# Attention and spectral layers on one core: the second addition behind the last low part, the norms' squares on ScalarE, wo's staging a step earlier

## The chip, the cores and the metric

The kernel runs on one core of a Trainium2 chip. A core has five engines that matter here: TensorE (PE in the profile; PEld is its weight load, which overlaps the products), VectorE (DVE), ScalarE (ACT), GpSimd (POOL) and SyncE (SP), which here issues nearly all DMA transfers. Each engine works its own instructions off in order and waits on semaphores for the others. The metric is the time of one execution on the device, in microseconds (us).

## The reference

The input x is 2048 x 1024 (one batch), and four blocks are applied to it, each with a residual: attention, spectral, attention, spectral.

```python
def _A_ref(x, wqkv, wo):                       # 32 heads of 32
    qkv = (x @ wqkv).reshape(B, S, 3, H, Dh)   # then q, k, v
    scores = einsum("bhqd,bhkd->bhqk", q, k) * Dh ** -0.5
    p = softmax(scores)
    return einsum("bhqk,bhkd->bhqd", p, v).reshape(B, S, D) @ wo
def _B_ref(x, w_r, w_i):
    return irfft2(rfft2(x) * (w_r + 1j * w_i), s=(S, D))
x = x + _A_ref(_layernorm(x), wqkv, wo)
x = x + _B_ref(_layernorm(x), w_r, w_i)
x = x + _A_ref(_layernorm(x), wqkv, wo)
x = x + _B_ref(_layernorm(x), w_r, w_i)
```

## The kernel before

The change touches the attention block, which is run twice (layer 0 and layer 1). Values that need more than 16 bits are kept as two halves of type f16: the high part, a rounded copy (ScalarE, line 167), and the low part, the rest (VectorE, line 168). The function `split` makes both. A product of two such values takes three products on TensorE.

The 32 heads are taken in 8 groups g of 4 heads. For a group, the queries stand in 4 chunks c of 512 and the keys in 16 tiles kt of 128, so that the loop over u = (c, kt) has 64 steps a group. A step does this:

- `S`: 12 score products (line 552) into two score tiles named s. The pool of score tiles has three buffers, which are taken in turn; besides S, the sum z at a chunk's end (line 581) and the norms' product (line 354) take one.
- two exponentials on ScalarE (line 556) of 128x1024 each, from s into p; p has eight buffers.
- on even steps `PV` (line 562) for the last two steps' p.
- `add` for one step: two additions on VectorE (line 575; at kt = 1 the form of line 573), which add p into two accumulators. They are late by a pair of steps.
- at a chunk's end `fin`: z from the accumulators on TensorE (line 581), then a transpose, a reciprocal and a scaling on VectorE (582 to 588); some steps later `out`: a cast on ScalarE (594), a subtraction on POOL (595) and a store to od on SP (597).
- on odd steps a piece of the filler: the projections for the next groups. `qk_chunk` makes a chunk of queries or keys: 24 products (line 337) into the projection buffer named x, of which there is one, then `split` into Q, or into K, which lies in the tile that the profile names R. `v_tiles` (line 381) makes v in the same buffer. So the next chunk's first product waits for both halves of the last one's split.

The exponentials' bias comes from a bound on the scores: each q or k chunk is squared (line 341, on POOL, into sq), and when four chunks are done `norms` sums the squares over a head's rows on TensorE (line 354, into a score buffer), VectorE takes the maximum (line 356, into mqk), and POOL works the bias out from it.

The weights of the next projection are loaded beside (line 248, into wst, three buffers) and split (into wqk or wv); in layer 0 alone VectorE also takes their largest value (lines 257 and 258). In group 6 wo is loaded and split in 16 pieces through the same three buffers (`load_wo`, line 417).

The order on TensorE and ScalarE in the loop is the order in which the code is written (`manual_schedule`). On VectorE, POOL and SP a scheduler sets the order. The name R stands for one large region that holds keys, values and the accumulators, and big for another one with the normalised input and wo.

## Time and profile before

| | |
|---|---|
| median of 3 runs | 3925.26 us (3918.09 to 3928.21) |
| profiled execution | 3923.33 us, span 3921.4 us |
| mean clock of TensorE | 0.984 |
| attention loop of layer 0, without its end | about 135 to 1300 us |
| attention loop of layer 1, without its end | about 2100 to 3240 us |

The page's first part gives each engine's busy time and its share of the span. A view of windows gives the same for a stretch of time, with the clock that TensorE was granted in it (PEclk, 1 is full speed). A view of waits names, for an engine, the line that waited, the engine and line it waited for, the sum, the number and the longest. In a timeline a row has the start, the duration, the engine, the line and operation with tile names (out<-in) and the number of instructions; in brackets the engine's idle time before it and what ended it. SPq is SP's queue, on which a row is the issue of a transfer.

### The profile page before, as it was taken

The page shows a single profiled execution, that of the slowest core. Times are in us where ns is not written, and L with a number is a line of the kernel's source. Part 1 is how long each engine was busy: PE and PEld are TensorE (multiplying, and loading weights), DVE is VectorE, ACT ScalarE, POOL GpSimd, SP SyncE. Part 2 cuts the span into 40 slices and gives each one's busy share as a digit, 9 for nine tenths or more (in the row PEclk, how much of TensorE's full clock was granted, in tenths as well). Part 3 has the DMA queues.
Part 4 walks back from the last instruction along what each step waited for, and adds up shares of the span by engine and source line. Part 5 has one row for each costly group of instructions (what it writes and reads, how often), then busy time and mean ns, then how long its engine had stood idle before and what let it go on. Part 6 is the DMA issues. An engine that isn't in the chain of part 4 may idle for free.

```text
span 3921.4 us, 79594 instructions
## 1 busy us (share of the span) xinstructions
PE 3742.8 (95%) x32948; PEld 1641.1 (42%) x32948; DVE 3183.4 (81%) x3781; ACT 2894.6 (74%) x3561; POOL 639.2 (16%) x575
## 2 busy tenths in 40 slices
PE   6999999999999999989989999999999999999798
PEld 4322432342234233368853334233422432333698
DVE  6689898989898887866666998899898888788455
ACT  4677887888788765557756888888888787665486
POOL 1111011101110200014321220122021102000143
PEclk9999999999999999999999999999999999999899
DMA  8000000000000211144170000000000002111333
GB/s 202 15 17 18 12 12 17 17 12 20 12 23 7 75 67 68 60 145 137 61 172 15 17 17 12 12 17 25 7 18 17 17 12 90 57 68 55 131 113 107
DMA packets 165142, 194.08 MB, mean 49 GB/s; under 512 B 74784, under 2 KB 120480, under 8 KB 163744
## 3 DMA queue, kind: packets, MB, share of 16 engines
q1 hardware_dynamic: 164624, 188.82, 15.4%
q8 instruction: 260, 4.26, 0.4%
q14 instruction: 114, 0.93, 0.1%
q10 hardware_dynamic: 144, 0.07, 0.0%
HBM read 123.83 MB, written 48.23 MB: 44 GB/s over the span
## 4 chain that ended last, share of the span: by engine, by line


## 5 line engine op out<-in xcount | busy, mean ns | idle before, releaser
L556 ACT ACTIVATE p<-s,bias 128x1024 f32<-128x1024 f32 x2048 | 2168.3, 1111 | 593.1 <-PE s L552 581.6
L575 DVE TENSOR_TENSOR R<-R,p 128x1024 f32<-128x1024 f32 x1792 | 2145.9, 1250 | 150.8 <-ACT p L556 146.7
L562 PE MATMUL o<-p,R 128*32 128x512 f32 x8192 | 985.1, 598 | 0.0
L337 PE MATMUL x<-big,wqk 128*128 128x512 f16 x2880 | 693.1, 387 | 28.0 <-DVE R L168 13.9
L552 PEld LDWEIGHTS <-R 32*128 32x128 f16 x12288 | 231.3, 92 | 782.1 <-issue 666.0
L337 PEld LDWEIGHTS <-wqk 128*128 128x128 f16 x3072 | 279.4, 99 | 472.0 <-issue 183.4
L552 PE MATMUL s<-R 32*128 32x512 f16 x6144 | 432.4, 379 | 19.3 <-ACT p L556 15.8
L552 PE MATMUL s<-Q,R 32*128 32x512 f16 x6144 | 432.9, 378 | 11.3 <-ACT p L556 10.6
L562 PEld LDWEIGHTS o<-p,R 128*32 128x32 f32 x8192 | 213.7, 109 | 524.5 <-issue 523.9
L595 POOL TENSOR_TENSOR ohl<-zt,ohl 128x512 f16<-128x512 f32 x62 | 180.0, 2903 | 1472.3 <-ACT ohl L594 1472.3
L381 PE MATMUL x<-wv,big 128*128 128x256 f16 x2688 | 325.7, 278 | 45.8 <-DMA big<-hl 33.2
L381 PEld LDWEIGHTS <-big 128*128 128x128 f16 x3072 | 294.4, 99 | 150.5 <-issue 77.7
L573 DVE SCALAR_TENSOR_TENSOR R<-p 128x1024 f32<-128x1024 f32 x128 | 153.9, 1203 | 198.8 <-ACT p L556 198.5
L341 POOL TENSOR_TENSOR sq<-R 128x512 bf16<-128x512 f16 x96 | 144.8, 1508 | 694.5 <-ACT R L167 691.3
L440 PE MATMUL x<-big 128*128 128x512 f16 x1008 | 228.0, 380 | 0.0
L440 PEld LDWEIGHTS <-big 128*128 128x128 f16 x1344 | 126.7, 98 | 177.6 <-issue 35.4
L885 DVE TENSOR_TENSOR H<-G,H 128x512 f16<-128x512 f32 (+1 forms) x68 | 47.4, 697 | 103.3 <-ACT H L884 103.2
L837 PE MATMUL ps<-cbi,H 128*128 128x256 f16 (+1 forms) x792 | 100.4, 275 | 6.1 <-ACT H L884 3.8
L830 ACT COPY U<-ps 64x256 f32<-64x256 f32 (+1 forms) x272 | 97.0, 357 | 8.5 <-PE ps L837 3.4
L830 ACT COPY B<-ps 64x256 f32<-64x256 f32 (+1 forms) x272 | 97.0, 356 | 6.7 <-PE ps L837 2.4
L341 POOL TENSOR_TENSOR sq<-Q 128x512 bf16<-128x512 f16 x32 | 44.9, 1403 | 323.8 <-ACT Q L167 323.8
L837 PE MATMUL ps<-cb,big 128*128 128x256 f16 x780 | 96.3, 273 | 0.0
(417 smaller groups left out, 3017.2 us busy)
## 6 DMA issues: line engine op xcount, KB each, us to landing
wst<-in_wp SPq DMA_DIRECT2D x96, 256.0 KB, 3.1
R<-y SPq DMA_DIRECT2D x32, 512.0 KB, 5.3
w<-in_w SPq DMA_DIRECT2D x60, 256.0 KB, 2.6
od<-ohl SPq DMA_DIRECT2D x56, 256.0 KB, 2.4
big<-od SPq DMA_DIRECT2D x16, 896.0 KB, 7.0
y<-R SPq DMA_DIRECT2D x20, 512.0 KB, 2.6
R<-in_x SPq DMA_DIRECT2D x16, 512.0 KB, 5.3
wst<-in_wo SPq DMA_DIRECT2D x32, 256.0 KB, 3.0
```

Source lines behind the costliest of these rows:

```text
L337: nc.tensor.matmul(ps, a, b, start=d == 0 and i == 0, stop=d == 7 and i == 2)
L341: nc.gpsimd.tensor_tensor(nrm[ph][:, c], t[:, 0], t[:, 0], op=ALU.mult)
L381: nc.tensor.matmul(ps[:, j], l, r, start=d == 0 and i == 0, stop=d == 7 and i == 2)
L440: nc.tensor.matmul(p, a, b, start=start and d == ds[0] and i == 0, stop=stop and d == ds[-1] and i == 2)
L552: nc.tensor.matmul(s[h // 2][:, h % 2], K[g][r, a, kt * 128:kt * 128 + 128], Q[g][r, b, c * 512:c * 512 + 512], start=i == 0, stop=i == 2)
L556: nc.scalar.activation(p, s[hf], AF.Exp, bias=bias[g], scale=SCALE / (SQ * SQ))
L562: nc.tensor.matmul(O[g, c][32 * h:32 * h + 32], V[g][:, kt, 32 * h:32 * h + 32], P[g, c, kt, h // 2][:, h % 2], start=kt == 0, stop=kt == ...
L573: nc.vector.scalar_tensor_tensor(acc[hf], P[g, c, 0, hf], 1e-34, p, op0=ALU.add, op1=ALU.add)
L575: nc.vector.tensor_add(acc[hf], acc[hf], p)
L595: eng.tensor_tensor(t[:, 1], r, t[:, 0], op=ALU.subtract)
L830: nc.scalar.copy(ov[64 * r:64 * r + 64, a0:a0 + m, x], tl[64 * x:64 * x + 64, :m, r])
L837: nc.tensor.matmul(out, l, r, start=k == 0, stop=k == len(mm_) - 1)
```

## The change

Three things are done in the attention loop.

1. `split` returns its VectorE instruction, and `qk_chunk` keeps it in the list lows. On odd steps, `add` is recorded under `issue_after` with the last of them: the two additions of that step stand behind the last low part in VectorE's order. No semaphore is added by that, since both are on VectorE.
2. The squares of line 341 are made on ScalarE with the activation Square, directly behind the chunk's high part. 56 of them stand in each layer's loop and 8 in each layer's prologue, 128 in all.
3. `load_wo` loads three pieces before its first yield, and one call of it is made when four chunks of filler are left, ahead of the calls that split.

```diff
 def split(nc, hi, lo, src, scale):
     nc.scalar.activation(hi, src, AF.Copy, scale=scale)
-    nc.vector.scalar_tensor_tensor(lo, src, scale, hi, op0=ALU.mult, op1=ALU.subtract)
+    return nc.vector.scalar_tensor_tensor(lo, src, scale, hi, op0=ALU.mult, op1=ALU.subtract)
...
-        split(nc, t[:, 0], t[:, 1], ps, SQ / (SX * SW))
-        nc.gpsimd.tensor_tensor(nrm[ph][:, c], t[:, 0], t[:, 0], op=ALU.mult)
+        lows.append(split(nc, t[:, 0], t[:, 1], ps, SQ / (SX * SW)))
+        nc.scalar.activation(nrm[ph][:, c], t[:, 0], AF.Square)
...
         load(0)
         load(1)
+        load(2)
+        yield
         for i in range(16):
-            load(i + 2)
+            if i:
+                load(i + 2)
...
-    left, parts, rests = 16, 20, list(range(12))
+    left, parts, rests = 17, 20, list(range(12))
...
                 for w in late[:1]:
-                    add(*w)
+                    with tc.issue_after(lows[-1].ins) if kt % 2 else ExitStack():
+                        add(*w)
...
+                if g == NG - 2 and todo == 4 and left == 17:
+                    next(lwo)
+                    left -= 1
```

What this makes of the order is seen at three places. The line numbers of the changed kernel are up to 8 higher: 573, 575 and 594 become 576, 578 and 597, and 556 and 566 become 559 and 569.

VectorE in layer 0, where the loop goes over from keys to v (386 us in the trace of before). wv is the weights' low part, wm and fw the largest value of the weights, R<-x the low part of the last key chunk, mqk the maximum of the norms. Before:

```order
L575 TENSOR_TENSOR R<-R,p 128x1024 x4
L168 SCALAR_TENSOR_TENSOR wv<-wst,wv 128x4x128 x2
L575 TENSOR_TENSOR R<-R,p 128x1024 x2
L257 TENSOR_REDUCE wm<-wst 128x1 x2
L258 TENSOR_TENSOR fw<-fw,wm 128x1 x2
L575 TENSOR_TENSOR R<-R,p 128x1024 x6
L168 SCALAR_TENSOR_TENSOR R<-x,R 128x512
L575 TENSOR_TENSOR R<-R,p 128x1024 x2
L356 TENSOR_REDUCE mqk<-s 128x1
L575 TENSOR_TENSOR R<-R,p 128x1024 x14
```

and after the change:

```order
L578 TENSOR_TENSOR R<-R,p 128x1024 x4
L168 SCALAR_TENSOR_TENSOR wv<-wst,wv 128x4x128 x2
L578 TENSOR_TENSOR R<-R,p 128x1024 x2
L257 TENSOR_REDUCE wm<-wst 128x1 x2
L258 TENSOR_TENSOR fw<-fw,wm 128x1 x2
L578 TENSOR_TENSOR R<-R,p 128x1024 x4
L168 SCALAR_TENSOR_TENSOR R<-x,R 128x512
L578 TENSOR_TENSOR R<-R,p 128x1024 x4
L356 TENSOR_REDUCE mqk<-s 128x1
L578 TENSOR_TENSOR R<-R,p 128x1024 x14
```

The low part has moved ahead of two additions; mqk has as many additions ahead of it as before.

VectorE in layer 0, in a group's query chunks (243 us in the trace of before). Before:

```order
L168 SCALAR_TENSOR_TENSOR wqk<-wst,wqk 128x512 x2
L575 TENSOR_TENSOR R<-R,p 128x1024 x2
L257 TENSOR_REDUCE wm<-wst 128x1 x2
L258 TENSOR_TENSOR fw<-fw,wm 128x1 x2
L575 TENSOR_TENSOR R<-R,p 128x1024 x6
L168 SCALAR_TENSOR_TENSOR Q<-x,Q 128x512
L575 TENSOR_TENSOR R<-R,p 128x1024 x8
L168 SCALAR_TENSOR_TENSOR Q<-x,Q 128x512
L575 TENSOR_TENSOR R<-R,p 128x1024 x2
L356 TENSOR_REDUCE mqk<-s 128x1
```

and after the change:

```order
L168 SCALAR_TENSOR_TENSOR wqk<-wst,wqk 128x512 x2
L578 TENSOR_TENSOR R<-R,p 128x1024 x2
L257 TENSOR_REDUCE wm<-wst 128x1 x2
L258 TENSOR_TENSOR fw<-fw,wm 128x1 x2
L578 TENSOR_TENSOR R<-R,p 128x1024 x4
L168 SCALAR_TENSOR_TENSOR Q<-x,Q 128x512
L578 TENSOR_TENSOR R<-R,p 128x1024 x8
L168 SCALAR_TENSOR_TENSOR Q<-x,Q 128x512
L578 TENSOR_TENSOR R<-R,p 128x1024 x4
L356 TENSOR_REDUCE mqk<-s 128x1
```

Again each low part stands two additions earlier, and mqk where it stood.

ScalarE in layer 0 around a chunk's end (oc and ohl belong to the output of a chunk of queries; 332 us in the trace of before is the place of the cast and the high part behind it). Before:

```order
L566 COPY oc<-o 128x512
L556 ACTIVATE p<-s,bias 128x1024 x2
L167 ACTIVATE R<-x 128x512
L556 ACTIVATE p<-s,bias 128x1024 x8
L594 CAST ohl<-zt 128x512
L167 ACTIVATE R<-x 128x512
L556 ACTIVATE p<-s,bias 128x1024 x4
```

and after the change:

```order
L569 COPY oc<-o 128x512
L559 ACTIVATE p<-s,bias 128x1024 x2
L167 ACTIVATE R<-x 128x512
L341 ACTIVATE sq<-R 128x512
L559 ACTIVATE p<-s,bias 128x1024 x8
L597 CAST ohl<-zt 128x512
L167 ACTIVATE R<-x 128x512
L341 ACTIVATE sq<-R 128x512
L559 ACTIVATE p<-s,bias 128x1024 x4
```

Each high part has a square directly behind it and ahead of the exponentials. On SP the loop's rows, the loads of wo among them, stand in the same order before and after; in layer 0's prologue one load of weights has moved ahead of two transposing transfers.

## The prediction

> **What bounds the kernel now.** I read the page's busy times first, then TensorE's busy time and clock over the attention loops of the two layers, then what TensorE waited for there, then the timeline at the longest waits.

> ```profile
> PE 3742.8 (95%) x32948; PEld 1641.1 (42%) x32948; DVE 3183.4 (81%) x3781; ACT 2894.6 (74%) x3561; POOL 639.2 (16%) x575
> core 0: us, PE busy (x) PEld busy (x) DVE busy (x) ACT busy (x) POOL busy (x), PEclk, DMA share, GB/s
> 28.00:135.00 107.00, 94.18 (x623) 58.29 (x624) 49.15 (x103) 42.97 (x59) 12.79 (x16) 0.95 0.55 116
> 135.00:1300.00 1165.00, 1144.01 (x10732) 400.17 (x10728) 1045.96 (x1055) 938.86 (x997) 140.37 (x100) 0.99 0.05 15
> 2100.00:3240.00 1140.00, 1129.79 (x10738) 397.05 (x10740) 1021.64 (x987) 939.95 (x999) 197.01 (x101) 1.00 0.05 16
> ```

> TensorE sets the time: in layer 0's loop it stands still 21 of 1165 us, in layer 1's 10 of 1140. VectorE is 90% and ScalarE 81% busy there, so both have room on average, and little of it locally. What can be won is TensorE's idle time and its clock. Layer 0's idle time, in the loop's window, and layer 1's, from 2080 to 3640 us:

> ```profile
> PE x L337 <- DVE R L168: 6.6, 3, 2.5
> PE x L337 <- DVE Q L168: 6.4, 3, 2.2
> PE x L381 <- DVE R L168: 6.0, 3, 2.0
> PE s L552 <- DVE mqk L356: 0.6, 1, 0.6
> PE s L354 <- ACT p L556: 0.6, 3, 0.2
> ...
> PE s L552 <- ACT p L556: 13.1, 13, 6.7
> PE s L354 <- POOL sq L341: 6.5, 3, 2.2
> PE s L552 <- DVE mqk L356: 2.6, 4, 0.7
> ```

> Layer 0 waits nine times, 19.0 us in all, for a low part (L168) of the single projection buffer x: three times each for a key part (R), a query part (Q), and a key part ahead of v's projection (L381). Layer 1 hardly has that wait, since its weights aren't measured by L257; it waits three times for POOL's squares. One low-part place, around 243 us:

> ```profile
> 234.75 7.74 DVE L575 TENSOR_TENSOR R<-R,p 128x1024 f32<-128x1024 f32 x6
> 237.80 0.60 ACT L167 ACTIVATE Q<-x 128x512 f16<-128x512 f32 x1
> 242.41 0.68 DVE L168 SCALAR_TENSOR_TENSOR Q<-x,Q 128x512 f16<-128x512 f32 x1
> 243.14 4.39 PE L337 MATMUL x<-big,wqk 128*128 128x512 f16 x12 [2.19 <-DVE Q L168]
> ...
> 243.10:246.50 3.40, 3.36 (x8) 1.13 (x8) 3.40 (x4) 0.01 (x1) 0.00 (x0) 0.50 0.02 5
> 1127.20:1130.60 3.40, 3.40 (x22) 1.08 (x24) 3.40 (x4) 0.73 (x1) 1.07 (x1) 0.51 0.00 0
> ```

> The high part is there at 238.40, the low part stands behind six additions of 1.29 us and ends at 243.09. TensorE loses 2.19 us and then runs a stretch of 3.40 us at half clock, which costs another 1.7. Seven of the nine places have such a stretch (the first and the last are shown): 11.9 us, which is the 0.01 that the window's mean clock of 0.99 lacks on 1165 us.

> **Part 1, the low part ahead of two additions.** By the order, the low part moves ahead of one step, two additions of about 1.25 us, so 2.5 us: as much as the longest of the nine waits. All nine go as waits for L168. What is late next is the maximum of the norms, L356, which keeps its place among the additions; it frees a score buffer that the next S wants. Its price is seen at such waits above: 0.6 and 2.6 us in 1 and 4 times, at most 0.7 each.

> Key and query chunks of layer 0 (six places): 6.6 + 6.4 idle and five half-clock stretches of 1.7 come back, 21.5 in all; three of them then run into L356 at 0.7, so 19.4 us. Bounds: 21.5 if L356 is never late, 10 if it takes the whole of the three query places (6.4 and three stretches).

> The three places ahead of v's projection come out otherwise:

> ```profile
> 381.49 2.12 ACT L556 ACTIVATE p<-s,bias 128x1024 f32<-128x1024 f32 x2
> 383.99 0.40 PE L354 MATMUL s<-sq,bones 128*32 128x512 bf16 x4
> 385.69 0.68 DVE L168 SCALAR_TENSOR_TENSOR R<-x,R 128x512 f16<-128x512 f32 x1
> 386.29 2.34 DVE L575 TENSOR_TENSOR R<-R,p 128x1024 f32<-128x1024 f32 x2
> 386.42 3.57 PE L381 MATMUL x<-wv,big 128*128 128x256 f16 x16 [2.03 <-DVE R L168]
> 388.56 0.68 DVE L356 TENSOR_REDUCE mqk<-s 128x1 f32<-128x512 f32 x1
> 389.92 0.83 PE L552 MATMUL s<-Q,R 32*128 32x512 f16 x12
> ```

> With the low part early L381 begins at 384.4, but the S behind it needs the buffer of L356, which ends at 389.24 whether the low part stands before or behind the two additions. S began at 389.92, so about 0.6 us is won at each place, 1.8 in all, of 6.0 and two stretches (9.4). Bounds 0 and 9.4; I take the low value, because both rows are on VectorE and their sum stays.

> Each addition moved is later by 0.68 us. The additions' readers are the exponentials that take their buffer (eight of them, four pairs' halves deep) and the sum z of a chunk; no row above shows an exponential waiting for an addition, so I cost that at nothing. If the cover went, it would be 0.68 at a chunk's end.

> **Part 2, squares on ScalarE.** 128 operations leave POOL. Three waits of layer 1 go:

> ```profile
> 2338.13 2.02 POOL L341 TENSOR_TENSOR sq<-R 128x512 bf16<-128x512 f16 x1
> 2340.20 0.38 PE L354 MATMUL s<-sq,bones 128*32 128x512 bf16 x1 [2.16 <-POOL sq L341]
> 2341.15 0.68 DVE L356 TENSOR_REDUCE mqk<-s 128x1 f32<-128x512 f32 x1
> ```

> That is 6.5 us and one half-clock stretch, 8.2. Behind it S meets L356 again, at 0.7 three times; and at three places of layer 1 the low part, by the order, now waits for its high part with the additions behind it, and they push L356 by about as much: 8.2 - 2.1 - 2.1 = 4.0. Bounds: 8.2, and -2 if L356 takes it all.

> The price is on ScalarE. A square is not in the trace there; the nearest row is a cast of the same tile, 0.62 us, and I take 0.6. It stands behind the high part and ahead of the exponentials, so those end 0.6 us later until ScalarE has made it up. Who waits for them: S and the norms' product, which take the score buffers (three).

> ```profile
> L594 ACT CAST ohl<-zt 128x512 f16<-128x512 f32 x64 | 39.5, 617 | 0.0
> ...
> 333.18 3.25 ACT L556 ACTIVATE p<-s,bias 128x1024 f32<-128x1024 f32 x3
> 334.46 0.82 PE L552 MATMUL s<-Q,R 32*128 32x512 f16 x12
> ```

> Where a high part stands alone, TensorE has 0.38 us before L354: the exponentials end at 383.61, L354 starts at 383.99. With 0.6 it loses 0.22. Twelve norms in each loop, some with less room: I take 0.24 each, 24 of them, 5.8 us. Where the cast of the output stands beside the high part, the first exponential ends at 334.27 (a third of 3.25 after 333.18) and the S begins at 334.46, with 0.16 left for its second buffer: it loses 0.44, six times a layer, 5.4 us. For the remaining 76 I cost them at nothing: ScalarE is idle 226 of the loop's 1165 us, six times the 34 us of a loop's 56 squares, and makes a square up before it is missed; if that cover goes, it is rival 2. Near wo's splits ScalarE has no room: 1.3 for two more. So 12.5 us is lost. Bounds: 0, and 0.6 for each of the 112 of the loops, 67 us, if ScalarE's 0.6 us always come through; I stay near the low end, since the rows above leave 0.16 us or more at each kind of place.

> **Part 3, wo's staging.** One load is issued a step earlier. At the place that hurts:

> ```profile
> 1277.81 0.95 SPq L417 DMA_DIRECT2D wst<-in_wo  x2
> 1322.89 6.67 SPq L417 DMA_DIRECT2D wst<-in_wo  x4
> ...
> 1344.74 9.31 POOL L595 TENSOR_TENSOR ohl<-zt,ohl 128x512 f16<-128x512 f32 x1 [9.80 <-ACT ohl L594]
> 1352.96 0.68 DVE L168 SCALAR_TENSOR_TENSOR Q<-x,Q 128x512 f16<-128x512 f32 x1
> 1354.08 0.38 SPq L597 DMA_DIRECT2D od<-ohl  x1
> 1354.55 0.91 SPq L417 DMA_DIRECT2D wst<-in_wo  x2
> 1357.62 0.63 ACT L167 ACTIVATE big<-wst 128x512 f16<-128x512 f32 x1 [6.88 <-DMA wst<-in_wo]
> 1359.30 1.46 PE L552 MATMUL s<-R 32*128 32x512 f16 x10 [6.95 <-ACT p L556]
> ```

> The first three loads were issued 40 us before the fourth anyway; by the order, SP's rows and the splits of wo stay what they were. The wait of 6.95 us (6.7 in layer 1) comes otherwise: POOL's subtraction takes 9.31 us beside the additions and ends at 1354.05, just behind a low part; the store of od waits for it on SP's queue, the later load of wo waits behind that store, ScalarE's split for the load, and the exponentials stand behind the split. The load itself is worth 0 here (at most 0.9, its issue time). But part 1 moves the low part at 1352.96 ahead of two additions, and I let the subtraction end 2.2 us earlier with it: twice 2.2, 4.4 us. Bounds: 0, and 13.7 and two half-clock stretches (17) if the wait goes.

> **Prologue.** Sixteen squares beside 43 us of ScalarE in 107: bounds -2 and 9.6 (all on the path); I take 1 us lost.

> **The sum.** 19.4 + 1.8 + 4.0 + 4.4 - 12.5 - 1 = 16.1 us. The profiled execution took 3923.33 us (span 3921.4), 1.9 under the median of 3925.26. 3923.3 - 16.1 = 3907 us.

> **A rule on the clock.** The rows show a half-clock stretch of 3.4 us behind waits of only 2 us. [...] As a rival: stretches stay, six of them for 10.2 us, time 3917. Chance 0.05.

> **The rivals.**
> 1. L356 takes over the query places and layer 1's whole: the gain falls by 9 and 6, to about 3921. For it: 90% of VectorE, and L356 keeps its place. Against: at most 0.7 us was ever waited for it. Chance 0.18.
> 2. Slower: the square delays exponentials by its length at every chunk, and S waits each time. 112 x 0.6 = 67 lost against 28.6 won otherwise (19.4 + 1.8 + 4.0 + 4.4 - 1): 3923 + 38 = 3962; at half of that price, 3928. It decides from 0.26 us a square on (28.6 / 112), or 0.36 for slower by over 0.3%. For it: high part and square come in a row, 1.2 us ahead of two exponentials of 2.12. Against: the three score buffers. Chance 0.15.
> 3. All waits go: no L356 behind the low part, wo's wait gone with its stretches, squares hidden: 19.0 + 11.9 + 8.2 + 17 = 56 off, 3867; with half the squares' price 3873. Against: L356 did not move. Chance 0.13.
> 4. The change does not do what it says (the low part still waits for its high part): 3923. Against: high parts end 4 us before low parts begin at 243 us. Chance 0.04.

> **How the numbers follow.** My forecast, some 3893 to 3915, has 0.45. 0.3% is 12 us, about what a measurement of this kernel can tell from no change, so faster means under 3913.5. Faster: nearly all of the forecast (0.43) and rival 3 (0.13), 0.56. Same: the rest of it, rivals 1 and 4 and the clock rule, 0.29. Slower: rival 2, 0.15. The range takes rival 3 in nearly to its end and rival 2 up to the half price and a little: 3876 to 3934.

> **What would show it.** Right: no wait of x for L168 above 0.5 us in layer 0, PEclk there 1.00, waits of S for mqk at some nine to twelve places of 0.7, L354's wait for POOL gone and replaced by 0.2 to 0.4 for exponentials, the load of wo landing 2 us earlier and the wait behind it 4.7 instead of 6.95. Wrong: waits of S for p at each chunk (rival 2), mqk waits of 2 us (rival 1), additions that exponentials wait for.

## The result and the profile after

The changed kernel takes 3925.12 us (median of 12 runs, 3921.78 to 3928.68); the kernel before, run beside it, 3925.32 (12 runs). The ratio is 1.0007, with a 95% interval of 1.0000 to 1.0015: no change that can be measured. The forecast was 3907. The profiled execution has a span of 3925.2 us.

The page and the two windows of the loops, after:

```profile
PE 3750.5 (96%) x32948; PEld 1644.3 (42%) x32948; DVE 3128.1 (80%) x3781; ACT 2964.6 (76%) x3689; POOL 448.9 (11%) x447
...
135.00:1300.00 1165.00, 1145.23 (x10760) 400.86 (x10756) 1022.67 (x1056) 967.18 (x1050) 74.76 (x49) 1.00 0.05 15
2100.00:3240.00 1140.00, 1131.62 (x10696) 398.46 (x10696) 992.42 (x982) 962.25 (x1046) 101.02 (x49) 1.00 0.05 16
```

POOL has lost 190 us of work and ScalarE has gained 70; layer 0's clock has gone from 0.99 to 1.00. TensorE stands still nearly as long as before (20 and 8 us in the two windows, against 21 and 10). What it waits for is another thing (first layer 0's loop, then layer 1 from 2080 to 3640 us):

```profile
PE s L555 <- DVE mqk L356: 10.2, 9, 2.3
PE s L584 <- DVE R L578: 4.5, 4, 1.6
PE s L584 <- ACT p L559: 2.4, 2, 1.2
PE s L555 <- ACT p L559: 1.3, 6, 0.4
PE s L354 <- ACT p L559: 1.0, 6, 0.2
...
PE s L555 <- ACT p L559: 14.6, 23, 4.6
PE s L555 <- DVE mqk L356: 7.7, 11, 1.0
...
PE s L354 <- ACT p L559: 1.3, 8, 0.2
```

All nine waits for L168 in layer 0 are gone, 19.0 us, and POOL's three in layer 1, 6.5 us. In their place stand waits of S for the norms' maximum mqk (0.6 before, now 10.2, in layer 0), and waits of the sum z (L584) for the additions and for the exponentials from which it takes its score buffer, 6.9 us. VectorE's own waits, which a reader would not look at while VectorE is not the bound, show what changed; the first row is of before, then layer 0 and layer 1 after:

```profile
DVE R L168 <- ACT R L167: 0.8, 3, 0.3
```

```profile
DVE R L168 <- ACT R L167: 36.2, 23, 2.3
...
DVE zt L585 <- PE s L584: 22.7, 13, 2.7
DVE Q L168 <- ACT Q L167: 8.9, 9, 1.7
...
DVE R L168 <- ACT R L167: 42.0, 29, 2.3
...
DVE zt L585 <- PE s L584: 22.7, 13, 2.7
DVE Q L168 <- ACT Q L167: 14.6, 12, 2.2
```

A low part that is placed ahead of two additions stands at the head of VectorE's queue before ScalarE has made its high part, and VectorE idles: 45 us at 32 places in layer 0 and 57 us at 41 in layer 1, where it had idled under 1. The order has a second effect of this kind. At 13 chunk ends in each of the two windows the first additions of the next chunk, which stood ahead of z's transposition, stand behind a low part now; the transposition is at the head of the queue instead, and VectorE idles 22.7 us for z. VectorE's idle time as a whole rose less, from 119 to 142 us in layer 0's window and from 118 to 148 in layer 1's, since it waits less for exponentials (108 us before and 65 after in layer 0); what has changed is where it stands idle. One such place in a group's second chunk, and the z behind it, after:

```profile
160.27 0.69 DVE L168 SCALAR_TENSOR_TENSOR R<-x,R 128x512 f16<-128x512 f32 x1 [1.28 <-ACT R L167]
...
174.14 2.10 PE L584 MATMUL s<-R,ones 128*32 128x512 f32 x8 [0.94 <-DVE R L578]
```

VectorE loses 1.28 us at 160; the chunk's last additions, which VectorE meets 12 us later behind the splitting and measuring of the weights, are late, and z waits 0.94 us where it had started without idle time. Some of z's waiting is hidden in its own row: its eight products take 1.06 us where nothing holds them and 2.10 here. In layer 1, where no wait of z is listed, its products took 34.1 us in all before and take 38.0 now.

### The profile page after: what moved, and what is told of

The parts are those of the page before. It is cut to its first block, busy times and chain, and to the rows that moved or that the text cites. A ratio compares the mean times of both kernels' runs of the same rounds, so it can differ in the third digit from the quotient of the medians.

```text
span 3925.2 us, 79400 instructions
## 1 busy us (share of the span) xinstructions
PE 3750.5 (96%) x32948; PEld 1644.3 (42%) x32948; DVE 3128.1 (80%) x3781; ACT 2964.6 (76%) x3689; POOL 448.9 (11%) x447
## 4 chain that ended last, share of the span: by engine, by line
## 5 line engine op out<-in xcount | busy, mean ns | idle before, releaser
L578 DVE TENSOR_TENSOR R<-R,p 128x1024 f32<-128x1024 f32 x1792 | 2090.6, 1225 | 121.6 <-ACT p L559 117.9
L337 PE MATMUL x<-big,wqk 128*128 128x512 f16 x2880 | 682.4, 382 | 7.6 <-ACT wqk L167 5.4
L337 PEld LDWEIGHTS <-wqk 128*128 128x128 f16 x3072 | 276.0, 98 | 445.4 <-issue 150.9
L598 POOL TENSOR_TENSOR ohl<-zt,ohl 128x512 f16<-128x512 f32 x62 | 165.5, 2669 | 2456.4 <-ACT ohl L597 2456.4
L381 PE MATMUL x<-wv,big 128*128 128x256 f16 x2688 | 322.3, 276 | 39.6 <-DMA big<-hl 33.2
L381 PEld LDWEIGHTS <-big 128*128 128x128 f16 x3072 | 293.4, 99 | 139.6 <-issue 67.9
L168 DVE SCALAR_TENSOR_TENSOR R<-x,R 128x512 f16<-128x512 f32 x88 | 60.6, 689 | 99.2 <-ACT R L167 99.2
L167 ACT ACTIVATE R<-x 128x512 f16<-128x512 f32 x88 | 52.7, 599 | 56.1 <-PE x L337 55.7
```

The lines of the kernel that those rows point to most:

```text
L168: return nc.vector.scalar_tensor_tensor(lo, src, scale, hi, op0=ALU.mult, op1=ALU.subtract)
L337: nc.tensor.matmul(ps, a, b, start=d == 0 and i == 0, stop=d == 7 and i == 2)
L381: nc.tensor.matmul(ps[:, j], l, r, start=d == 0 and i == 0, stop=d == 7 and i == 2)
L578: nc.vector.tensor_add(acc[hf], acc[hf], p)
L598: eng.tensor_tensor(t[:, 1], r, t[:, 0], op=ALU.subtract)
```

## The experiments

My theory after this comparison, called A (C in the later runs, with what the first ones had added): part 1 costs by VectorE's idle time at the head of its queue. Its rival B: the squares on ScalarE eat what part 1 wins. Each run is compared with runs of the kernel before on the same chip. Differences in us are between the two medians; the ratio is worked out from all runs of both kernels, and the two can differ by some 5 us (for part 1 alone the medians are 22 us apart, and 0.0068 is 27).

**Each part alone.** Part 1 alone is the change without the edits of line 341 and of `load_wo`:

```diff
-                    add(*w)
+                    with tc.issue_after(lows[-1].ins) if kt % 2 else ExitStack():
+                        add(*w)
```

> Part 1 alone (squares stay on POOL, wo's loads as before). Theory A (head of the queue): the low part now stands at the head of VectorE's queue and VectorE idles there for the high part, 45 us in layer 0's loop and 57 in layer 1's of the changed kernel; the additions behind it come late and with them the maximum mqk and the sum z. Then these waits stand here too, with the squares on POOL: layer 0 wins 19.0 of waits and 11.9 of clock and loses about 9.6 (mqk), 6.9 (z) and 5 (clock), layer 1 loses about 5 and keeps POOL's 6.5, the wait at wo shrinks by 2.4 in each layer: net about -9, 3916. Theory B (the squares on ScalarE eat the gain): no z wait, few mqk waits, 19.4 + 1.8 + 4.4 - 2 = 24 won: 3902.

Measured: 3948.56 us, ratio 1.0068 (1.0055 to 1.0081), 22 us slower. Its waits of TensorE in layer 0's loop, and two of VectorE's:

```profile
PE s L552 <- DVE mqk L356: 13.9, 9, 2.9
PE s L581 <- DVE R L575: 5.0, 4, 1.4
PE x L337 <- DVE R L168: 4.1, 3, 1.4
PE x L381 <- DVE R L168: 3.1, 3, 2.2
PE x L337 <- DVE Q L168: 3.1, 3, 1.0
PE s L581 <- ACT p L556: 2.6, 2, 1.3
...
DVE R L168 <- ACT R L167: 26.4, 17, 2.3
...
DVE Q L168 <- ACT Q L167: 8.7, 9, 1.8
```

B falls: the z and mqk waits stand here with the squares on POOL. A's waits are there, but its 3916 is missed by 32 us: half of the waits for the low part stay as well (10.3 of 19.0), and layer 1 waits 14.2 us for mqk.

Part 2 alone:

```diff
-        nc.gpsimd.tensor_tensor(nrm[ph][:, c], t[:, 0], t[:, 0], op=ALU.mult)
+        nc.scalar.activation(nrm[ph][:, c], t[:, 0], AF.Square)
```

> Part 2 alone. Theory A: POOL's waits of layer 1 go (6.5 and a half-clock stretch, less 2 for mqk), the additions beside POOL's squares get shorter by 0.3 and the low parts of layer 0 come some 0.4 earlier at nine places, and ScalarE's price is about 10 to 12: net between 0 and +4, 3925 to 3929; nine waits for L168 of 1.6 to 2.1 stay in layer 0. Theory B: the whole gain of part 1 (24) is eaten here, 3940 or more, with waits of S for exponentials at many chunks.

Measured: 3903.98 us, ratio 0.9950 (0.9938 to 0.9962), 22 us faster. Both theories missed it.

```profile
PE x L337 <- DVE Q L168: 3.6, 3, 1.3
PE x L337 <- DVE R L168: 3.4, 3, 1.9
PE s L354 <- ACT p L556: 2.4, 10, 0.4
PE x L381 <- DVE R L168: 2.1, 3, 0.7
PE s L552 <- DVE mqk L356: 1.9, 3, 0.6
```

With VectorE's order untouched, the nine waits for the low part fall from 19.0 to 9.1 us, and not one half-clock stretch is left in the loop, where seven were (the loop's clock is 1.00 instead of 0.99). So the squares on POOL were a cause of the low parts' lateness. POOL's three waits of layer 1 are gone as well. In the profiled executions layer 0, from its first exponential to its last, is 14.9 us shorter than before, and layer 1 is 3.8 shorter. The price on ScalarE is there too (2.4 us for L354 instead of 0.6), and smaller than what is won. Parts 1 and 2 alone, +22 and -22, add up to the change's zero; that this is no rule, the pairs below show.

Part 3 alone (the call of `load_wo` at four chunks, not printed here, is in it):

```diff
+        load(2)
+        yield
         for i in range(16):
-            load(i + 2)
+            if i:
+                load(i + 2)
```

> Part 3 alone. Both theories: the loads were issued 40 us ahead of the first split anyway and SP's order is the same, so 0: within 1 us of before, and the wait of 6.95 at the wo place unchanged.

Measured: 3926.17 us, ratio 0.9999 (0.9990 to 1.0008). The wait of S at the wo place, in a window from 1320 to 1400 us, of this kernel:

```profile
PE s L555 <- ACT p L559: 6.7, 1, 6.7
```

It stays, and part 3 is worth nothing.

**Half the dose of part 1.** Only the second addition of the odd step, and the next step's two, stand behind the low part, so that it moves ahead of one addition; squares on POOL.

```diff
-    def add(g, c, kt):
+    def add(g, c, kt, low=None, first=0):
         for hf in range(2):
+            with tc.issue_after(low.ins) if low is not None and hf >= first else ExitStack():
...
-                    add(*w)
+                    low = lows[-1] if kt % 2 else low
+                    add(*w, low, kt % 2)
```

> Part 1 at half its dose: only the second half of the odd step's addition and the next step's stand behind the low part, so it moves ahead of one addition, not two (squares on POOL, wo as before). Theory A: VectorE's idle time for high parts falls to a third or less, the z wait goes and mqk waits shrink to 1 at v and 0 to 0.3 elsewhere; the waits for L168 in layer 0 fall from 2.1 to about 0.9 each and most half-clock stretches go with them: 8 + 3 + 3 left of 30.9, about 3908, faster than the full dose. Theory B: between before and part 1 alone, about 3913.

Measured: 3916.66 us, ratio 0.9983 (0.9975 to 0.9992). The sign of the dose turns: one addition wins 10 us (7 by the ratio), two lose 22. VectorE idles 15 us for high parts in layer 0 instead of 35. The size is A's missed by 9 us, since 12.9 us of waits for L168 stayed and mqk and z took 9.8.

**The price of a square on either engine.** The squares of the first three of four chunks are made twice, once on ScalarE (on top of part 2) and once on POOL (on top of the kernel before). The second writes the same values, and nobody waits for it alone.

```diff
+        for _ in range(2 if c < 3 else 1):
+            nc.scalar.activation(nrm[ph][:, c], t[:, 0], AF.Square)
```

> Part 2 alone, with every square of the first three of four chunks made twice on ScalarE (42 more of 0.6 us in each loop; the second writes the same values). If the price of a square is its delay of the exponentials less the 0.15 to 0.4 us of room at the score buffers, a second one finds no room: 84 times some 0.4, 3904 + 35 = 3939. If ScalarE's idle time takes squares up however they fall: 3904 + 3.

Measured: 3941.71 us, ratio 1.0042 (1.0028 to 1.0055): 38 us above part 2 alone, 0.45 for each of the 84 squares more in the loops (12 more stand in the prologues), as expected. S waits for exponentials much more often (layer 0, then layer 1 with the wo place):

```profile
PE s L553 <- ACT p L557: 9.4, 23, 0.8
...
PE s L553 <- ACT p L557: 25.0, 39, 6.4
```

That is 17 us more than in part 2 alone (1.3 and 15.7 us there); the rest of the 38 isn't listed as a wait for exponentials.

> The kernel before, with every square of the first three of four chunks made twice on POOL (no consumer waits for the second). Theory C, that POOL's squares cost by slowing VectorE's additions beside them: each second square costs VectorE 0.3 to 0.6 us, 84 of them, the low parts of layer 0 are later by 0.5 to 1 us at nine places and the wait at wo gets longer: +8 to +15, 3934 to 3941. If only the latency of the last square mattered (POOL's waits of layer 1): 0, 3926.

Measured: 3960.14 us, ratio 1.0095 (1.0081 to 1.0110), 36 us slower, more than twice the expected size. The waits in layer 0 and the page's row of the additions:

```profile
PE x L337 <- DVE R L168: 12.5, 6, 4.2
PE x L337 <- DVE Q L168: 11.5, 3, 4.0
PE x L382 <- DVE R L168: 6.7, 3, 2.4
...
L576 DVE TENSOR_TENSOR R<-R,p 128x1024 f32<-128x1024 f32 x1792 | 2189.2, 1274 | 147.4 <-ACT p L557 143.2
```

The same row of before, and of part 2 alone:

```profile
L575 DVE TENSOR_TENSOR R<-R,p 128x1024 f32<-128x1024 f32 x1792 | 2145.9, 1250 | 150.8 <-ACT p L556 146.7
```

```profile
L575 DVE TENSOR_TENSOR R<-R,p 128x1024 f32<-128x1024 f32 x1792 | 2107.6, 1227 | 170.5 <-ACT p L556 167.1
```

So a square on POOL costs VectorE's additions: 38 us less of them without the squares, 43 us more with 96 of the 128 squares doubled, while VectorE's order in the two loops is the same in all three kernels. That a mean moves by 23 ns says little; what decides is that a square follows a high part, and so its delay falls on the additions just ahead of that chunk's low part, which TensorE waits for. At the place of 243 us the six additions ahead of the low part took 7.74 us in the kernel before, where one square ran on POOL beside them. The same six in part 2 alone, with no square on POOL, and in this kernel, with two:

```profile
233.68 6.90 DVE L575 TENSOR_TENSOR R<-R,p 128x1024 f32<-128x1024 f32 x6
...
237.51 8.58 DVE L576 TENSOR_TENSOR R<-R,p 128x1024 f32<-128x1024 f32 x6
```

Each square costs VectorE 0.84 us there. The six take 6.90 us with no square on POOL, 7.74 with one and 8.58 with two; by what the square makes them longer is not shown.

**Only the last square.**

```diff
+        if c == 3:
+            nc.scalar.activation(nrm[ph][:, c], t[:, 0], AF.Square)
+        else:
+            nc.gpsimd.tensor_tensor(nrm[ph][:, c], t[:, 0], t[:, 0], op=ALU.mult)
```

> Only the last of four chunks' squares on ScalarE, the others stay on POOL. By latency alone (POOL's waits of layer 1, 6.5 and a half-clock stretch) 8 won less some 3 for the squares at the norms: 3921. If most of part 2's gain of 22 is the additions' freedom from POOL, a quarter of that (4) comes on top at most: 3917 to 3921, and the nine low-part waits of layer 0 stay near 2 us. If the last square carries everything: 3904.

Measured: 3912.86 us, ratio 0.9969 (0.9958 to 0.9981), 11 us faster, half of part 2 with a quarter of its squares. The wait of v's product (L384 here, L381 before) fell from 6.0 to 2.7; the last key chunk's square stands just ahead of that low part. POOL's three waits of layer 1 went too, and that is the larger part: in the profiled executions layer 0, from its first exponential to its last, is 3.8 us shorter than before and layer 1 is 7.1. So the 11 us are not the additions' alone. The other query and key places stayed as they were:

```profile
PE x L337 <- DVE R L168: 6.7, 3, 2.7
PE x L337 <- DVE Q L168: 6.5, 3, 2.3
PE x L384 <- DVE R L168: 2.7, 3, 1.0
```

**Part 1 where it is wanted.** The order is asked for only at the nine places of layer 0 at which TensorE had waited (full dose, squares on POOL; the diff is against part 1 alone):

```diff
-                    with tc.issue_after(lows[-1].ins) if kt % 2 else ExitStack():
+                    with tc.issue_after(lows[-1].ins) if not layer and g < NG - 2 and u in ((25,) if g % 2 else (41, 61)) else ExitStack():
```

> Part 1 at the nine places of layer 0 alone where TensorE waited for the low part (two additions ahead, full dose); everywhere else VectorE's order is that of before; squares on POOL. The forecast's term for these places was 21.2 us. Theory C, that part 1 costs at the other places, where the high part is not there yet and VectorE idles for it: no idle of VectorE for high parts, hardly a z wait, so about 17 to 21 won, 3904 to 3908. If moving a low part ahead of two additions costs by itself (mqk and z late whatever the high part does): most of the gain is given back, 3918 or more.

Measured: 3906.65 us, ratio 0.9951 (0.9937 to 0.9964), 19 us faster, where the same dose everywhere was 22 slower. TensorE's waits for mqk and for z, and VectorE's for high parts, in layer 0:

```profile
PE s L552 <- DVE mqk L356: 7.5, 4, 2.9
PE s L581 <- DVE R L575: 1.1, 3, 0.6
...
DVE R L168 <- ACT R L167: 1.0, 3, 0.3
```

At these places VectorE was behind and the high part long there, and hardly anything is idle. No wait of VectorE for z is listed either. The 42 us between the two kernels are the price of the order at the other places, VectorE's idle time for high parts and for z together; the runs don't separate these two. Of these, the waits of TensorE account for 22 in layer 0 (mqk 13.9 against 7.5, z 7.6 against 1.1, the low part 10.3 against 0.9) and some 6 in layer 1 (mqk 14.2 against 2.6, POOL's squares 1.3 against 6.5, small ones); five half-clock stretches of 3.41 us against two (the loop's clock is 0.99 against 1.00) make some 5 more. The rest I can't place.

**Both together.** Part 2 with half of part 1, part 2 with part 1 at the nine places, and the last with the squares of three chunks made later (the diff is the third's edit to the second):

```diff
-        nc.scalar.activation(nrm[ph][:, c], t[:, 0], AF.Square)
+        if c < 3 and ph not in PH0:
+            squares.append((nrm[ph][:, c], t[:, 0]))
+        else:
+            nc.scalar.activation(nrm[ph][:, c], t[:, 0], AF.Square)
...
                 S(g, c, kt)
+                if squares and kt % 2:
+                    nc.scalar.activation(*squares.pop(0), AF.Square)
```

> Part 2 with half of part 1 (the low part ahead of one addition). Theory C: part 1 costs by VectorE's idle time at its queue's head, and what it can win is only the 9.1 us of waits for L168 that part 2 leaves in layer 0. The half dose wins most of those 9 and pays by mqk and z waits, 6 + 3 in layer 0 and 3 in layer 1, as it does with the squares on POOL: 3904 to 3910, not faster than part 2 alone. If the two parts added up as each was measured alone (-22 and -9): 3895.

Measured: 3900.53 us, ratio 0.9937 (0.9922 to 0.9952). It isn't told from part 2 alone by more than the intervals allow. Nor does this run tell whether the two effects add up: by the ratios they would make -26 us, and -25 was measured, with an interval of some 6 us to either side.

> Part 2 with part 1 at the same nine places. 9.1 us of waits for L168 are left there by part 2, no half-clock stretch hangs on them any more; they go, and mqk takes 0.6 to 0.9 at six of them: 3904 - 9 + 4 = 3899, ahead of part 2 alone and level with part 2 plus half of part 1. If part 1 and part 2 added up: 3904 - 19 = 3885.

Measured: 3898.36 us, ratio 0.9926 (0.9912 to 0.9939), some 28 us faster than both kernels of this case. In layer 0 no wait for L168 is listed any more, and mqk takes the 4 us that were expected, at three places instead of six:

```profile
PE s L552 <- DVE mqk L356: 4.0, 3, 1.4
```

Part 2 wins 22, part 1 at nine places 19, both 28: they cure the same nine waits.

> As the last, with the squares of the first three of four chunks made on ScalarE a pair of steps after their high part, behind the next pair's exponentials, instead of directly behind the high part. If the price of a square is that it stands in one row with a high part ahead of the exponentials, six waits of S for exponentials in each loop go (0.45 each, 5 in all): 3894. If the price is ScalarE's time as such: no change from the last.

Measured: 3898.27 us, ratio 0.9926 (0.9913 to 0.9940), no change from the last. In layer 0 the waits of S for exponentials left the list, as expected, 1.3 us, and from 2080 to 3640 us they fell from 15.6 to 12.7; the time that was to come with them didn't.

## Why the prediction was wrong

The time was to fall by 16 us and did not move. Split by parts, the forecast had part 1 win 23.5 us (19.4 + 1.8 + 4.4, less 2.1 in layer 1), and alone it lost 22; it had part 2 lose 7.4 (8.2 - 2.1 - 12.5 - 1), and alone it won 22. Both parts came out with the other sign, and that the sum is only 16 us off is luck: the two errors have opposite signs. By its steps:

- **The nine places** were priced at 21.2 us (19.4 + 1.8). Alone they gave 19. That step stands, and so does its split: at v's three places mqk took the wait over, as argued (7.5 us of waits for mqk in layer 0).
- **"no row above shows an exponential waiting for an addition, so I cost that at nothing"** is the step that failed, together with the low part that "now waits for its high part" at "three places of layer 1". I looked at who reads the additions, found room, and priced a move at the places where it helps. The order is asked for at every odd step. Elsewhere the high part isn't there, so VectorE idles (under 1 us before, 45 and 57 after), additions are late, and mqk and z with them: 10.2 and 6.9 us in layer 0, 7.7 for mqk in layer 1. The forecast had 2.1 for mqk in layer 0's query places, left another 4.2 to it at v's (6.0 - 1.8), had 4.2 more than before in layer 1, where 5.1 came, and nothing for z. It had no place either for z's transposition, for which VectorE idles 22.7 us in each window. With the squares on ScalarE the order everywhere costs 27 us against the order at nine places (3925 against 3898).
- **POOL's waits in layer 1** went, 6.5 us, as forecast.
- **The squares on ScalarE** were priced at 12.5 us. A square takes 0.63 us and the norms' product waits about 0.2 for exponentials, as worked out; in part 2 alone all waits for exponentials together grew by some 7.5 us. The rows are of the changed kernel:

```profile
2334.39 0.63 ACT L341 ACTIVATE sq<-R 128x512 bf16<-128x512 f16 x1
...
2337.08 0.40 PE L354 MATMUL s<-sq,bones 128*32 128x512 bf16 x4 [0.16 <-ACT p L559]
```

That the first square uses up the room at the score buffers is not shown: the doubled squares cost about what was expected of that, but squares moved behind the next exponentials won nothing, and no run takes the squares off POOL without putting them on ScalarE, so the price of the first stays unmeasured. What the sum left out is what part 2 gives VectorE. Its effect on the low parts (19.0 to 9.1 us, and all the half-clock stretches) was the same wait that part 1 was credited with, so it would not have raised the sum; it would have told that part 2 alone is worth some 14 us (9.9 + 11.9 - 7.4), nearly the whole forecast.
- **Part 3** is worth 0, as forecast. The wait at the wo place fell by 2.4 us, as forecast, by the earlier end of POOL's subtraction. It is part 1's doing: in part 1 alone the longest wait there is 4.7 us, in part 2 alone 6.9. The rows after:

```profile
1342.74 7.46 POOL L598 TENSOR_TENSOR ohl<-zt,ohl 128x512 f16<-128x512 f32 x1 [43.03 <-ACT ohl L597]
...
1355.14 1.46 PE L555 MATMUL s<-R 32*128 32x512 f16 x10 [4.54 <-ACT p L559]
```

Around it stand new ones: five waits for exponentials, the one of 4.5 among them, come to 6.3 us and one for mqk to 1.0, so that the 7.1 us of before in the window from 1320 to 1400 are 7.5 now.

- **The rivals.** The first (mqk takes over, 3921; its own terms give 3922) names a part of what happened; it lacked z and the cause. The fourth (3923) was nearest by number. It had the low parts still wait for their high parts, which came true at the places where nothing was to be won; it was set aside because "high parts end 4 us before low parts begin at 243 us": true there, and of no use for the other places. The slower one, squares that delay S at every chunk, came only with the squares doubled. The one on the clock, that half-clock stretches stay (3917), didn't hold: with the low-part waits they went, seven to two in layer 0.

## What to carry to other kernels

An order that is asked for at every step acts at every step: list all places where the moved instruction will stand, and at each compare when its input is ready with when the engine gets to it; VectorE isn't the bound here, and yet its 45 and 57 us of waiting at its queue's head made what stood behind late, with 10.2 us of TensorE's waits for mqk and 6.9 for z in layer 0. Before reordering an engine that is late, look for what slows its work there: taking the neighbour's work away was worth as much here (22 us against 19), and cost nothing in order. Two cures for one wait didn't add up (28 us together).

## What was not expected of the hardware

- POOL work that nobody waits for cost time: 84 more squares in the loops, 36 us, and VectorE's additions took 43 us more with 96 squares doubled.
- The clock fell behind some short waits, but not behind all. Before the change, waits of TensorE of 1.92 and 1.96 us were not followed by a half-clock stretch and those of 1.99 to 2.54 in layer 0 were; yet a wait of 2.16 at 2340.20 was not, nor one of 2.27 in the changed kernel at 1125.53. One of 2.09 us in the changed kernel was. The traces show in what the two differ. Before the change the seven stretches of layer 0 begin at 243.09, 304.53, 386.45, 615.14, 983.78, 1045.22 and 1127.14 us, which are 18, 24, 67, 108, 18 and 24 times 3.413 us apart: they lie on one raster, whose step is worked out from these starts (884.05 us from the first to the last, 259 steps). Cut at it, all 672 pieces of the two windows of before have a clock of 1.00 or 0.50 (664 and 8); of the changed kernel, whose raster goes through 383.57, they are 670 and 2. Three pieces of before and two of the changed kernel are:

```profile
239.68:243.09 3.41, 1.27 (x20) 0.32 (x13) 3.41 (x4) 2.91 (x3) 0.59 (x1) 1.00 0.00 0
2335.46:2338.88 3.42, 2.58 (x31) 0.58 (x24) 3.42 (x4) 2.92 (x4) 3.42 (x2) 1.00 0.00 0
2338.88:2342.29 3.41, 2.09 (x17) 1.49 (x16) 3.41 (x4) 0.99 (x1) 1.27 (x1) 1.00 0.23 77
...
383.57:386.98 3.41, 1.32 (x16) 0.38 (x17) 3.41 (x5) 0.49 (x1) 1.07 (x1) 1.00 0.00 0
386.98:390.39 3.41, 3.41 (x24) 0.73 (x20) 3.33 (x3) 1.63 (x2) 3.41 (x1) 0.50 0.00 0
```
